# Splitting batch 0 at query 192 so that FFN blocks start on its first tokens

## The chip, the cores and the metric

The kernel runs on one core of a Trainium2 chip. The metric is the device time of one execution in microseconds. A comparison is given as a ratio: the mean time of one kernel's fast runs over that of the other's fast runs of the same rounds, with a 95% interval. It is therefore not quite the ratio of the medians, which are quoted beside it. "Granted clock" is the share of TensorE's full rate that the chip grants at that moment; 0.5 is half clock.

The kernel before took 367.71 us in the rounds of the changed kernel. On the other chips that the experiments ran on, its medians were 367.65 to 368.13 and its single runs 367.04 to 368.56. Half a microsecond between kernels therefore means something only within the same rounds.

## The reference

Attention in a sliding window of 128 keys with a linear bias, over 8 batches of 576 tokens, 8 heads of 64; the outcome goes through a gated FFN (GELU of one product times another, then the output product).

```python
scores = np.matmul(q, k.transpose(0, 1, 3, 2)) / np.sqrt(D)
rel = pos[:, None] - pos[None, :]
mask = (rel >= 0) & (rel < 128)
scores = np.where(mask, scores + bias, -1e9)        # bias = -slope[h] * abs(rel)
attn = np.exp(scores - scores.max(-1, keepdims=True))
attn = attn / (attn.sum(-1, keepdims=True) + 1e-9)
x = np.matmul(attn, v) ...                          # [4608, 512]
out = (gelu(x @ w_gate) * (x @ w_val)) @ w_out      # d_ff = 1536
```

## The kernel before

Attention is computed transposed: keys on partitions, queries along the row. For a batch, ScalarE (ACT) takes the exponential of the scores in PSUM (the banks into which TensorE writes its results), VectorE (DVE) multiplies by a table with bias and window ("mask"). TensorE (PE) then makes the sums of the probabilities with a matrix of ones, DVE their reciprocals, PE spreads these over the heads' partitions, and PE multiplies with v. DVE writes the product of the values and the reciprocals to `xT`, which the FFN reads. The parts that the argument touches:

```python
def sums(b, s):                       # PE, then the reciprocal on DVE
    ...
    nc.vector.reciprocal(sumrow[b][:, lo:hi], ps[:, 0:hi - lo])

def values(b, s, cs):                 # PE, then the product that FFN reads
    ...
        nc.vector.tensor_tensor(out=xT[...], in0=ps[:, 0:hi - lo],
                                in1=recip[b][:, c, lo:hi], op=ALU.mult)

def gate_val(g, f, lo=0, hi=512):     # one FFN block: 128 of the 1536 columns
    pg, pv = bank(), bank()
    ... 8 matmuls of hi - lo columns ...
    nc.scalar.activation(out=gl, in_=pg, func=AF.Gelu)
    nc.vector.tensor_tensor(out=hid[g][:, f, lo:hi], in0=pv, in1=gl, op=ALU.mult)
```

Batch 0 cannot hide behind FFN work, as there is none yet. The kernel before cuts it at query 320 (cut where marked):

```python
first((0, 1))                                       # transposes of head pairs 0, 1
scores(0, 0, (0, 1), lambda: first((2,)))
first((3,))
scores2(0)
scores(0, 0, (2, 3), lambda: rest((0, 1), dve))
scores(0, 1, (0, 1), lambda: sums(0, 0))
rest((2, 3), act)
scores(0, 1, (2, 3))
spread_pe(0, 0)
values(0, 0, range(4))
sums(0, 1)
for f in range(2):
    gate_val(0, f, 0, 320)
spread_pe(0, 1)
gate_val(0, 2, 0, 320)
values(0, 1, range(4))
for f in range(3):
    gate_val(0, f, 320, 512)
...                                                 # blocks 3 to 11 on 512 columns
```

The softmax here doesn't subtract the row's maximum and nothing guards it: scores larger than these inputs give would overflow.

## Time and profile before

| What | Kernel before |
|---|---|
| time, median | 367.71 us |
| PE busy over the span | 95% |
| granted clock full again from | 23.6 us |
| first FFN matmul | 23.3 us |
| last mask of batch 0 ends | 21.1 us |
| second reciprocal | 23.45 to 25.2 us |
| batch 1 keys transposed on PE | 41.98 us |

From FFN block 8 on, both kernels do the same work in the same order, and PE transposes batch 1 between the blocks. In the profiled run of the kernel before, 367.3 us minus 41.98 is 325.3 us.

In the timelines, a line gives the start and the length in us, engine, source line, operation, output and input, and the count of merged instructions. In brackets stands the idle time of that engine before it and what ended it.

### The profile page before, as it was taken

To read this page: it belongs to the slowest core of one execution; us is meant where nothing else is said; L and a number is where in the kernel's file an instruction comes from. 1 tells how busy PE (TensorE), PEld (TensorE's weight loads), DVE (VectorE), ACT (ScalarE), POOL (GpSimd) and SP (SyncE) were. 2 spreads that over 40 slices of the span, in tenths; PEclk is the share of its full clock that TensorE was granted. 3 is DMA by queue.
4 is the path that set the end of the run, shared out by engine and by line. 5 is a ranking of instruction groups with operands and counts; after the bars stand their busy time and mean duration, and the time that the engine had idled before them with its cause. 6 is when DMAs were issued, how large, how long until landed. Compare 5 with 4: busy or idle time off the path is not lost.

```text
span 365.5 us, 6601 instructions
## 1 busy us (share of the span) xinstructions
PE 347.8 (95%) x2614; PEld 171.3 (47%) x2656; DVE 188.6 (52%) x306; ACT 187.3 (51%) x339; POOL 107.9 (30%) x140
## 2 busy tenths in 40 slices
PE   3799999999999999999999999999999999999995
PEld 2455545444454445444445444444444444444442
DVE  4794448543695469475547454655564404302320
ACT  5863487434966376943783368436842223323321
POOL 8945859913519202900850040000000000000000
PEclk9779999999999999999999999999999999999999
DMA  9999999999969994999991992094205020011002
GB/s 103 136 199 178 177 163 184 174 153 200 162 116 121 136 92 81 143 103 217 127 196 50 228 97 89 33 221 53 87 32 131 0 109 7 0 60 58 0 29 88
DMA packets 151168, 41.41 MB, mean 113 GB/s; under 512 B 138816, under 2 KB 144448, under 8 KB 151136
## 3 DMA queue, kind: packets, MB, share of 16 engines
q0 software_dynamic: 112608, 18.88, 67.8%
q1 hardware_dynamic: 38528, 22.10, 27.2%
q8 instruction: 21, 0.34, 0.4%
q14 instruction: 11, 0.09, 0.1%
HBM read 42.47 MB, written 9.51 MB: 142 GB/s over the span
## 4 chain that ended last, share of the span: by engine, by line
PE 86%; ACT 5%; DVE 3%; DMA 3%; issue 1%; POOL 1%; POOLq 0%; SPq 0%; ACTq 0%; DVEq 0%
PE ps L281 50%; PE ps L297 23%; PE ps L262 4%; ACT P L170 4%; PE ps L163 4%; DMA qT<-qs 3%; PE ps L221 2%; PE ps L244 2%; DVE r L230 1%; DVE P L173 1%; DVE xT L268 1%; ACT emask L346 1%; PE ps L142 1%; POOL ks L104 0%; ACT L170 0%
## 5 line engine op out<-in xcount | busy, mean ns | idle before, releaser
L286 DVE TENSOR_TENSOR hT<-ps,gelu 128x512 bf16<-128x512 f32 (+2 forms) x111 | 74.3, 674 | 121.9 <-PE ps L281 109.3
L285 ACT ACTIVATE gelu<-ps 128x512 bf16<-128x512 f32 (+2 forms) x111 | 64.9, 585 | 119.6 <-PE ps L281 117.2
L281 PE MATMUL ps<-xT,wg 128*128 128x512 bf16 (+2 forms) x430 | 110.6, 374 | 0.8
L281 PE MATMUL ps<-xT,wv 128*128 128x512 bf16 (+2 forms) x435 | 110.4, 373 | 0.6
L297 PE MATMUL ps<-wo,hT 128*128 128x512 bf16 x413 | 97.2, 380 | 1.5 <-issue 0.6
L170 ACT ACTIVATE P<-ps 128x512 bf16<-128x512 f32 x144 | 74.4, 632 | 7.1 <-PE ps L163 7.0
L281 PEld LDWEIGHTS <-wv 128*128 128x128 bf16 x444 | 43.3, 98 | 50.3 <-issue 0.2
L281 PEld LDWEIGHTS <-wg 128*128 128x128 bf16 x444 | 41.9, 98 | 48.9 <-issue 1.1
L173 DVE TENSOR_TENSOR P<-P,emask 128x1024 bf16<-128x1024 bf16 x72 | 48.3, 685 | 31.3 <-ACT P L170 31.0
L297 PEld LDWEIGHTS <-hT 128*128 128x128 bf16 x432 | 39.8, 98 | 49.0 <-issue 4.4
L84 POOL DMA_DIRECT2D vb<-in_v_dram x40 | 33.7, 862 | 75.8 <-PE ps L262 75.0
L302 ACT COPY osb<-ps 128x512 f32<-128x512 f32 x36 | 21.7, 603 | 37.2 <-PE ps L297 32.8
L84 POOL DMA_DIRECT2D qs<-in_q_dram x35 | 29.6, 877 | 24.9 <-DMA qT<-qs 12.9
L230 DVE RECIPROCAL r<-ps 128x320 f32<-128x320 f32 (+1 forms) x16 | 30.7, 1939 | 3.1 <-PE ps L221 3.1
L84 POOL DMA_DIRECT2D ks<-in_k_dram x35 | 29.6, 887 | 6.4 <-DMA qs<-in_q_dram 3.0
L163 PE MATMUL ps<-qT,kT 64*128 64x256 bf16 (+1 forms) x384 | 24.0, 254 | 3.0 <-DVE kT L136 1.3
L268 DVE TENSOR_TENSOR xT<-ps,rb 128x320 bf16<-128x320 f32 (+1 forms) x64 | 24.7, 449 | 0.8 <-DMA rb<-rd 0.8
L163 PEld LDWEIGHTS <-kT 64*128 64x128 bf16 x384 | 13.1, 96 | 16.9 <-issue 11.6
L262 PE MATMUL ps<-P,vb 128*64 128x128 bf16 (+2 forms) x384 | 19.4, 251 | 0.1
L262 PEld LDWEIGHTS <-vb 128*64 128x64 bf16 x384 | 15.4, 113 | 7.3 <-issue 7.2
L221 PE MATMUL ps<-P,ones 128*32 128x128 bf16 (+2 forms) x384 | 11.6, 256 | 1.3 <-DVE P L173 1.3
L221 PEld LDWEIGHTS <-ones 128*32 128x32 bf16 x384 | 8.5, 101 | 5.6 <-issue 4.5
(47 smaller groups left out, 91.3 us busy)
## 6 DMA issues: line engine op xcount, KB each, us to landing
out_dram<-osb SPq DMA_DIRECT2D x36, 256.0 KB, 2.7
rb<-rd SPq DMA_DIRECT2D x8, 576.0 KB, 7.1
vb<-in_v_dram POOLq DMA_DIRECT2D x32, 128.0 KB, 4.7
qs<-in_q_dram POOLq DMA_DIRECT2D x28, 128.0 KB, 6.7
ks<-in_k_dram POOLq DMA_DIRECT2D x28, 128.0 KB, 6.4
wg<-in_moe_w_gate_dram POOLq DMA_DIRECT2D x4, 384.0 KB, 11.0
wv<-in_moe_w_val_dram POOLq DMA_DIRECT2D x4, 384.0 KB, 12.2
wo<-in_moe_w_out_dram POOLq DMA_DIRECT2D x2, 768.0 KB, 10.9
```

The lines of the kernel that those rows point to most:

```text
L84: nc.gpsimd.dma_start(out=t[lo:128, j, :].rearrange("p (h d) -> p h d", h=H), in_=src[b][:, 128 * j - 64 + lo:128 * j + 64, :].rearrange(" ...
L163: nc.tensor.matmul(out=ps[:, col:col + 128 * n].rearrange("p (n t) -> p n t", n=n), lhsT=blocks(kT, b, i, c, j, 1).rearrange("p n t -> p ( ...
L170: nc.scalar.activation(out=dst, in_=src, func=AF.Exp, scale=0.125)
L173: nc.vector.tensor_tensor(out=dst, in0=dst, in1=m, op=ALU.mult)
L221: nc.tensor.matmul(out=ps[32 * c:32 * c + 32, a:e], lhsT=ones[:, min(j, 1), i, :], rhs=prob(b, s, c, i, j, e - a), start=(i == 0 and j == ...
L230: nc.vector.reciprocal(sumrow[b][:, lo:hi], ps[:, 0:hi - lo])
L262: nc.tensor.matmul(out=ps[64 * i:64 * i + 64, a:e], lhsT=vb[b % 2][:, j, 64 * h:64 * h + 64], rhs=prob(b, s, c, i, j, e - a), start=(j == ...
L268: nc.vector.tensor_tensor(out=xT[:, c, b * S + lo:b * S + hi], in0=ps[:, 0:hi - lo], in1=recip[b][:, c, lo:hi], op=ALU.mult)
L281: nc.tensor.matmul(out=ps[:, 0:hi - lo], lhsT=w[:, c, 128 * f:128 * (f + 1)], rhs=xT[:, c, t0 + lo:t0 + hi], start=(c == 0), stop=(c == 3))
L285: nc.scalar.activation(out=gl[:, 0:hi - lo], in_=pg[:, 0:hi - lo], func=AF.Gelu)
L286: nc.vector.tensor_tensor(out=hid[g][:, f, lo:hi], in0=pv[:, 0:hi - lo], in1=gl[:, 0:hi - lo], op=ALU.mult)
L297: nc.tensor.matmul(out=po, lhsT=hid[g][:, f, 128 * t:128 * (t + 1)], rhs=wo[:, f, :], start=(f == 0), stop=(f == NF - 1))
```

## The change

Its intent is to bring FFN work to PE sooner. The first 192 tokens go through all of attention first; six FFN blocks run on these 192 columns while exponentials, masks and the reciprocal of the other 384 are made. Loads are reordered for it: 192 tokens' queries and keys, then the other 384, two pieces of v, half of the gate and value weights, the rest. The core of the diff:

```diff
-PART = ((0, 320), (320, 576))
+PART = ((0, 320), (320, 576), (0, 192), (192, 576))
...
-    RUNS = ((0, 128, 3), (384, 96, 2))
+    RUNS = ((0, 96, 2), (192, 128, 3))
...
+    for w in (0, 1):
+        transpose_runs(0, w, range(4), dve)
+    scores_first()
+    transpose_runs(1, 0, (0, 1), act)
+    transpose_runs(1, 1, (0, 1), act)
+    transpose_runs(1, 0, (2, 3), dve)
+    sums(0, 2)
+    transpose_runs(1, 1, (2, 3), act)
+    scores(0, 1, (0, 1), lambda: (spread_pe(0, 2, (dve, dve)), values(0, 2, range(4))))
     scores(0, 1, (2, 3))
-    spread_pe(0, 0)
-    values(0, 0, range(4))
-    sums(0, 1)
-    for f in range(2):
-        gate_val(0, f, 0, 320)
-    spread_pe(0, 1)
-    gate_val(0, 2, 0, 320)
-    values(0, 1, range(4))
-    for f in range(3):
-        gate_val(0, f, 320, 512)
+    scores2(0, 2)
+    scores2(0, 1)
+    later = []
+    for f in range(3):
+        gate_val(0, f, 0, 192, later)
+    sums(0, 3)
+    for tail in later:
+        tail()
+    for f in (3, 4):
+        gate_val(0, f, 0, 192)
+    spread_pe(0, 3)
+    gate_val(0, 5, 0, 192)
+    values(0, 3, range(4))
+    for f in range(6):
+        gate_val(0, f, 192, 512)
```

With `later`, GELU and product of blocks 0 to 2 are emitted behind the second reciprocal, so that they do not hold it up on DVE.

More of the change, by code (lines that the diff above doesn't have):

```diff
@@ L12 @@
 ENG = mybir.EngineType
-PART = ((0, 320), (320, 576))
+PART = ((0, 320), (320, 576), (0, 192), (192, 576))
 PIECES = (((0, 0, 192), (1, 64, 320), (2, 192, 320)),
-          ((2, 0, 128), (3, 0, 256), (4, 128, 256)))
-PCOL = ({0: 64, 1: 256}, {4: 0, 2: 128, 3: 256})
+          ((2, 0, 128), (3, 0, 256), (4, 128, 256)),
+          ((0, 0, 192), (1, 64, 192)),
+          ((1, 0, 128), (2, 0, 128), (2, 128, 256), (3, 128, 384), (4, 256, 384)))
+PCOL = ({0: 64, 1: 256}, {4: 0, 2: 128, 3: 256}, {0: 0, 1: 192})
 @with_exitstack
@@ L90, in load_qk, with load_run, load_v @@
         load(ks[b % 2], k, b)
-    RUNS = ((0, 128, 3), (384, 96, 2))
+    RUNS = ((0, 96, 2), (192, 128, 3))
     def runs(t, n):
         first, parts, r = RUNS[n]
-        lo = 1536 * n
+        lo = 1024 * n
         return t.rearrange("p j x -> p (j x)")[0:parts, lo:lo + 512 * r].rearrange(
             "p (h x) -> p h x", h=H)
-    def load_runs(n, h0, h1):
+    def load_run(n, t, src):
         first, parts, r = RUNS[n]
-        for t, src in ((qs[0], q), (ks[0], k)):
-            nc.gpsimd.dma_start(
-                out=runs(t, n)[:, h0:h1, :],
-                in_=src[0][h0:h1, first:first + parts * r, :].rearrange(
-                    "h (p r) d -> p h (r d)", r=r))
-    def load_v(b):
-        load(vb[b % 2], v, b)
+        nc.gpsimd.dma_start(
+            out=runs(t, n),
+            in_=src[0][:, first:first + parts * r, :].rearrange("h (p r) d -> p h (r d)", r=r))
+    def load_v(b, js=range(5)):
+        load(vb[b % 2], v, b, js)
     def load_w(lo, hi):
@@ L120, in by_pair, with transpose_runs @@
         return t.rearrange("p j c t -> p (j c t)").rearrange("p (c x) -> p c x", c=4)
-    def transpose_runs(n, what, c, ps):
+    def transpose_runs(n, what, cs, copy):
         first, parts, r = RUNS[n]
         src = runs((qs, ks)[what][0], n)
-        for x in range(r):
-            for i in (0, 1):
-                nc.tensor.transpose(
-                    out=ps[64 * i:64 * i + 64, parts * x:parts * x + parts],
-                    in_=src[:, 2 * c + i, 64 * x:64 * x + 64],
-                    identity=ident[0:parts, 0:parts])
-    def untangle(copy, n, what, c, ps):
-        first, parts, r = RUNS[n]
-        dst = by_pair((qT, kT)[what][0])[:, c, 64 + first:64 + first + parts * r]
-        copy(out=dst.rearrange("p (x r) -> p x r", r=r),
-             in_=ps[:, 0:parts * r].rearrange("p (r x) -> p x r", r=r))
+        ps = bank().bitcast(BF16)
+        for k, c in enumerate(cs):
+            for x in range(r):
+                lo = parts * (r * k + x)
+                for i in (0, 1):
+                    nc.tensor.transpose(
+                        out=ps[64 * i:64 * i + 64, lo:lo + parts],
+                        in_=src[:, 2 * c + i, 64 * x:64 * x + 64],
+                        identity=ident[0:parts, 0:parts])
+        for k in range(0, len(cs), 2):
+            lo = parts * r * k
+            dst = by_pair((qT, kT)[what][0])[
+                :, cs[k]:cs[k] + 2, 64 + first:64 + first + parts * r]
+            copy(out=dst.rearrange("p c (x r) -> p c x r", r=r),
+                 in_=ps[:, lo:lo + 2 * parts * r].rearrange("p (c r x) -> p c x r", c=2, r=r))
     def transpose(b, what, c, copy):
@@ L173, in mask, with scores2 @@
         nc.vector.tensor_tensor(out=dst, in0=dst, in1=m, op=ALU.mult)
-    def scores2(b):
+    def scores2(b, j=2):
         P = p2_pool.tile([128, 4, 2, 128], BF16, name="P2")
-        probs2[b] = P
+        probs2[b, j] = P
         ps = [bank(), bank()]
@@ L181, in scores2, with scores_first @@
             for i in (0, 1):
-                score(b, c, i, 2, 2, 1, ps[i], 128 * c)
+                score(b, c, i, j, 2, 1, ps[i], 128 * c)
         for i in (0, 1):
             exp(P[:, :, i, :], ps[i].rearrange("p (c n) -> p c n", c=4))
-        mask(P.rearrange("p c i n -> p (c i) n"), emask[:, :, 0:128])
+        lo = 128 * (2 - j)
+        mask(P.rearrange("p c i n -> p (c i) n"), emask[:, :, lo:lo + 128])
+    def scores_first():
+        pss = []
+        for c in range(4):
+            ps = [bank(), bank()]
+            pss.append(ps)
+            for j, a, e in PIECES[2]:
+                for i in (0, 1):
+                    col = PCOL[2][j]
+                    nc.tensor.matmul(
+                        out=ps[i][:, col:col + e - a],
+                        lhsT=by_pair(kT[0])[64 * i:64 * i + 64, c, 128 * j:128 * j + 128],
+                        rhs=by_pair(qT[0])[64 * i:64 * i + 64, c, 64 + a:64 + e],
+                        start=True, stop=True)
+        for c, ps in enumerate(pss):
+            P = p_pool[0].tile([128, 2, 512], BF16, name="P")
+            probs[0, 2, c] = P
+            for i in (0, 1):
+                exp(P[:, i, 0:320], ps[i][:, 0:320])
+            mask(P[:, :, 0:192], emask[:, 2 * c:2 * c + 2, 64:256])
+            mask(P[:, :, 192:320], emask[:, 2 * c:2 * c + 2, 0:128])
     def scores(b, s, cs, then=None):
@@ L206, in scores, with prob @@
                  emask[:, 2 * c:2 * c + 2, :].unsqueeze(2).to_broadcast((128, 2, 2, 256)))
-    def prob(b, s, c, i, j, n):
-        if (s, j) == (0, 2):
-            return probs2[b][:, c, i, 0:n]
-        return probs[b, s, c][:, i, PCOL[s][j]:PCOL[s][j] + n]
+    def prob(b, s, c, i, j, a, e):
+        if (s, j) == (0, 2) or (s == 3 and a == 0):
+            return probs2[b, j][:, c, i, 0:e - a]
+        t = min(s, 1) if s != 2 else 2
+        return probs[b, t, c][:, i, PCOL[t][j]:PCOL[t][j] + e - a]
     sumrow, recip = {}, {}
@@ L217, in sums @@
         ps = bank()
-        for j, a, e in PIECES[s]:
+        for n, (j, a, e) in enumerate(PIECES[s]):
             for i in (0, 1):
@@ L222, in sums @@
                         out=ps[32 * c:32 * c + 32, a:e],
-                        lhsT=ones[:, min(j, 1), i, :], rhs=prob(b, s, c, i, j, e - a),
-                        start=(i == 0 and j == 2 * s), stop=(i == 1 and j == 2 * s + 2),
+                        lhsT=ones[:, min(j, 1), i, :], rhs=prob(b, s, c, i, j, a, e),
+                        start=(i == 0 and n == 0), stop=(i == 1 and n == len(PIECES[s]) - 1),
                         skip_group_check=True)
-        if s == 0:
+        if b not in sumrow:
             sumrow[b] = r_pool.tile([128, S], FP32, name="r")
@@ L238, in spread_dma, with spread_pe @@
                 in_=d[:, i, :].unsqueeze(0).to_broadcast((64, 4, S)))
-    def spread_pe(b, s):
+    def spread_pe(b, s, copies=(nc.scalar.copy, nc.vector.tensor_copy)):
         lo, hi = PART[s]
@@ L249, in spread_pe @@
         for c, ps in enumerate(pss):
-            copy = nc.scalar.copy if c % 2 == 0 else nc.vector.tensor_copy
-            copy(out=recip[b][:, c, lo:hi], in_=ps[:, 0:hi - lo])
+            copies[c % 2](out=recip[b][:, c, lo:hi], in_=ps[:, 0:hi - lo])
     def values(b, s, cs):
@@ L258, in values @@
             pss.append(ps)
-            for j, a, e in PIECES[s]:
+            for n, (j, a, e) in enumerate(PIECES[s]):
                 for i in (0, 1):
@@ L264, in values @@
                         lhsT=vb[b % 2][:, j, 64 * h:64 * h + 64],
-                        rhs=prob(b, s, c, i, j, e - a),
-                        start=(j == 2 * s), stop=(j == 2 * s + 2), skip_group_check=True)
+                        rhs=prob(b, s, c, i, j, a, e),
+                        start=(n == 0), stop=(n == len(PIECES[s]) - 1),
+                        skip_group_check=True)
         for c, ps in zip(cs, pss):
@@ L272, with gate_val @@
     hid = {}
-    def gate_val(g, f, lo=0, hi=512):
+    def gate_val(g, f, lo=0, hi=512, later=None):
         if g not in hid:
@@ L283, in gate_val, with act @@
                     rhs=xT[:, c, t0 + lo:t0 + hi], start=(c == 0), stop=(c == 3))
-        gl = g_pool.tile([128, 512], BF16, name="gelu")
-        nc.scalar.activation(out=gl[:, 0:hi - lo], in_=pg[:, 0:hi - lo], func=AF.Gelu)
-        nc.vector.tensor_tensor(out=hid[g][:, f, lo:hi], in0=pv[:, 0:hi - lo],
-                                in1=gl[:, 0:hi - lo], op=ALU.mult)
+        def act():
+            gl = g_pool.tile([128, 512], BF16, name="gelu")
+            nc.scalar.activation(out=gl[:, 0:hi - lo], in_=pg[:, 0:hi - lo], func=AF.Gelu)
+            nc.vector.tensor_tensor(out=hid[g][:, f, lo:hi], in0=pv[:, 0:hi - lo],
+                                    in1=gl[:, 0:hi - lo], op=ALU.mult)
+        if later is None:
+            act()
+        else:
+            later.append(act)
     acc = {}
@@ L304, in out_half @@
             nc.sync.dma_start(out=out[r0:r0 + 128, :], in_=osb)
-    load_runs(0, 0, 4)
+    load_run(0, qs[0], q)
+    load_run(0, ks[0], k)
     nc.vector.memset(ident, 0.0)
@@ L314 @@
         base=0, pattern=[[-1, 128]], channel_multiplier=1)
-    load_runs(0, 4, 8)
+    load_run(1, qs[0], q)
     tmpl = consts.tile([128, 256], FP32, name="tmpl")
@@ L323 @@
             base=base, pattern=[[step, 128]], channel_multiplier=chan)
-    load_runs(1, 0, 8)
+    load_run(1, ks[0], k)
+    load_v(0, (0, 1))
+    step = DFF // 4
+    load_w(0, step)
     for c in range(4):
@@ L328 @@
             base=-32 * c, pattern=[[-16, 2], [0, 64]], channel_multiplier=1)
-    load_v(0)
-    step = DFF // 4
-    for n in range(4):
+    load_w(step, 2 * step)
+    load_v(0, (2, 3, 4))
+    for n in (2, 3):
         load_w(step * n, step * (n + 1))
@@ L350 @@
     act, dve = nc.scalar.copy, nc.vector.tensor_copy
-    def first(cs):
-        for w in (0, 1):
-            for c in cs:
-                ps = bank().bitcast(BF16)
-                transpose_runs(0, w, c, ps)
-                untangle(act if c == 3 else dve, 0, w, c, ps)
-    def rest(cs, copy):
-        for c in cs:
-            for w in (0, 1):
-                ps = bank().bitcast(BF16)
-                transpose_runs(1, w, c, ps)
-                untangle(copy, 1, w, c, ps)
-    first((0, 1))
-    scores(0, 0, (0, 1), lambda: first((2,)))
-    first((3,))
-    scores2(0)
-    scores(0, 0, (2, 3), lambda: rest((0, 1), dve))
-    scores(0, 1, (0, 1), lambda: sums(0, 0))
-    rest((2, 3), act)
-    scores(0, 1, (2, 3))
-    spread_pe(0, 0)
-    values(0, 0, range(4))
-    sums(0, 1)
-    for f in range(2):
-        gate_val(0, f, 0, 320)
-    spread_pe(0, 1)
-    gate_val(0, 2, 0, 320)
-    values(0, 1, range(4))
-    for f in range(3):
-        gate_val(0, f, 320, 512)
+    for w in (0, 1):
[7 more added lines that the diff above has]
+    scores(0, 1, (0, 1), lambda: (spread_pe(0, 2, (dve, dve)), values(0, 2, range(4))))
+    scores(0, 1, (2, 3))
+    scores2(0, 2)
+    scores2(0, 1)
+    later = []
+    for f in range(3):
+        gate_val(0, f, 0, 192, later)
[9 more added lines that the diff above has]
+        gate_val(0, f, 192, 512)
     for n in range(2):
@@ L426 @@
             load_v(g + 2)
-        for f in range(3 if g == 0 else 0, NF):
+        for f in range(6 if g == 0 else 0, NF):
             gate_val(g, f)
```

## The prediction

> **What bounds the kernel now.** I read the page's forty slices first, then the chain that ended last, then the timelines of TensorE, VectorE and GpSimd for the first 50 us, then the table of stretches with the granted clock, then the DMA issues.
>
> The forty slices (9.14 us each):
> ```profile
> PE   3799999999999999999999999999999999999995
> DVE  4794448543695469475547454655564404302320
> PEclk9779999999999999999999999999999999999999
> DMA  9999999999969994999991992094205020011002
> ```
> From slice 4 on PE is full at full clock; the change does not touch that work. What can be won lies in slices 1 to 4: PE waits, and PE at reduced clock.
>
> TensorE's timeline there (start, us, engine, line, operation, count, idle before):
> ```profile
> 17.51 1.06 PE L163 MATMUL ps<-qT,kT 64*128 64x128 bf16 x12 [0.16 <-ACT kT L136]
> 18.91 1.45 PE L244 MATMUL ps<-r,sel 32*128 32x320 f32 x8 [0.35 <-DVE r L230]
> 20.30 2.13 PE L262 MATMUL ps<-P,vb 128*64 128x192 bf16 x24
> 22.36 1.04 PE L221 MATMUL ps<-P,ones 128*32 128x128 bf16 x24
> ...
> 28.62 1.23 PE L281 MATMUL ps<-xT,wg 128*128 128x192 bf16 x4
> 29.69 0.49 PE L281 MATMUL ps<-xT,wv 128*128 128x192 bf16 x4
> ...
> 41.98 0.44 PE L142 MATMUL ps<-ident,ks 128*128 128x128 bf16 x5
> ```
> From 18.9 to 28.6 PE has no gap: three FFN blocks on 320 tokens (L281) fill the second reciprocal. The one gap is at 28.62, where PE waits for the last xT product: that product ends at 29.56, so I count the remaining FFN as starting at about 29.4. At 41.98 batch 1 is transposed.
>
> VectorE's timeline, the links between:
> ```profile
> 16.61 2.16 DVE L230 RECIPROCAL r<-ps 128x320 f32<-128x320 f32 x1 [1.21 <-PE ps L221]
> 23.45 1.76 DVE L230 RECIPROCAL r<-ps 128x256 f32<-128x256 f32 x1
> 28.15 1.41 DVE L268 TENSOR_TENSOR xT<-ps,rb 128x256 bf16<-128x256 f32 x4
> ```
> The reciprocal is 2.16 us for 320 columns and 1.76 for 256: 6.25 ns a column, so 1.36 us for 192 and 2.56 us for 384.
>
> Stretches (us, PE, PEld, DVE, ACT, POOL busy, clock, DMA share, GB/s):
> ```profile
> 12.00:14.00 2.00, 0.80 (x18) 0.50 (x13) 1.55 (x5) 2.00 (x5) 2.00 (x4) 0.84 1.88 120
> 20.00:22.00 2.00, 2.00 (x26) 1.60 (x24) 2.00 (x5) 1.85 (x4) 0.70 (x1) 0.50 1.26 189
> 23.00:24.00 1.00, 1.00 (x16) 0.58 (x9) 1.00 (x3) 0.00 (x0) 0.38 (x1) 0.70 1.32 204
> ```
> A clock of 0.84 over two us, with 0.50 after, puts the fall at 13.4; 0.70 over one us puts the rise at 23.6. For ten us PE ran at half clock: the twelve score matmuls at 17.51 took 1.06 us, the same twelve at 55.67 took 0.62.
>
> DMA issues of two of the last batch 1 key tiles (KB each, us to landing):
> ```profile
> ks<-in_k_dram POOLq DMA_DIRECT2D x2, 128.0 KB, 5.6
> ```
> The last of them is issued at 35.87, so it lands at about 41.5, just ahead of the 41.98 at which PE transposes it. The DMA queue is full all the way there.
>
> **What the Trainium skill says.** "TensorE: Matmul & The Clock Gate", Part 1: the HAM clock gate: half clock is the default, a busy window of about 3.4 us releases it, an idle one puts it back. The trace agrees on the sizes: the half-clock stretch of 10.2 us is three such windows. It also shows that less than an idle window suffices: at 13.4 the clock fell although PE was busy for roughly half of the window before. Same page, "Architectural detail", queue depths: PE may pull only weight loads ahead, ACT and DVE are strictly first in, first out. The timelines agree (instructions run in program order), and the argument below rests on it. "ScalarE: Activation LUTs", What ACT_TABLE_LOAD costs: about 1283 ns for the load; the trace has 1.28 us at 21.12, hidden. "DMA: Bandwidth & Descriptors", Specifications: line rate needs 512 B or more; the trace agrees in kind: the table of stretches has about 202 GB/s while weights come, 154 while 128-byte head rows of batch 1 do.
>
> **The change part by part.**
>
> 1. Loads. Equal bytes in another order, 192 tokens first. The first queries land at 4.97 now and should at about 5.2, the keys at 6.5 instead of 6.16 (smaller packets); the 384 tokens' keys land at about 11.6 (now 11.8). One issue of 0.76 us fewer ahead of the mask template lets the eight emask exponentials end at 7.6 instead of 8.3. Gate and value weights of the first quarter land near 18.4 instead of 22.2, the second quarter near 22.3 instead of 26.1, late v tokens near 24. These meet their readers.
>
> 2. First part. Scores of 192 tokens: eight exponentials of 320 columns at about 0.36 us (from 0.31 for 256 and 0.49 to 0.51 for 512) run 8.3 to 11.2, masks end at 11.7. PE then waits about 1.6 us for the keys of part two (11.6). Transposes, sums, transposes end at 14.1 at half clock; the VectorE copy of the transposed queries ends at 14.0; reciprocal 14.0 to 15.4; spread 15.4 to 16.4; values to 17.5; xT to 18.2.
>
> 3. Exponentials of part two. Twelve of 512 columns at 0.51 are 6.1 us, starting at 15.05 after the last ACT copy, with about 0.9 us idle while PE is in the spread and values: end at about 22.1, last mask at 22.8. Now the last mask ends at 21.1. So the first FFN starts early (first block at 19.1, now 23.3), but the last attention input comes later by 1.7.
>
> 4. Second part. sums(0, 3) needs that last mask with its first piece; it ends near 23.6 and the reciprocal of 384 columns runs 23.7 to 26.25, against 23.45 to 25.2 now. FFN blocks 0 to 2 have run (19.1 to 21.65), block 3 runs 23.5 to 24.15. Block 4 needs the PSUM bank of block 0's value half, which VectorE frees only after the reciprocal, as its three products stand behind it: bank free at 26.6. The spread stands behind block 4 on PE: 26.6 + 0.65 (block 4: eight matmuls of 192 columns at 0.082) + 1.1 (spread: 0.71 for 256 columns, so 1.07 for 384) + 0.65 (block 5) + 1.4 (values: 768 streamed columns a head for 512 in the 24 matmuls that took 1.07 at 27.56, with some 0.2 of fixed tail) + 0.6 (last product) = 31.0.
>
> 5. The balance. At that point six blocks of 192 = 1152 columns are done, against three of 320 = 960. The difference, 192 columns by eight matmuls at 2.4 columns a ns (512 columns step by 0.216 us), is 0.64 us. So the remaining FFN starts 31.0 - 0.2 (the same overlap as now) - 29.4 = 1.4 later with 0.64 less to do: **a loss of 0.8 us** at full clock.
>
> 6. The clock. PE is dense from about 15.4, so the window 16.8 to 20.2 can release the clock at 20.2 rather than 23.6; the working above includes it. But PE is idle about 1.2 us before sums and 2.4 us before block 4. The window 23.6 to 27.0 would have it busy for about a third; at 13.4 about a half was not enough. If it throttles, spread, block 5 and values run at half clock until 30.4: about 1.5 us more, **a loss of 2.3**. I hold this for as likely as not.
>
> **The rivals.**
>
> A, the intended gain. If my half-clock estimates for 11 to 19 us are too long, or block 4's bank comes free early, the remaining FFN starts at 28.5 to 29.5: a gain of 0.5 to 1.5. For it: the present PE spends ten us at half clock, and dense FFN work sooner is what releases it. Against: the chain of steps 2 to 4 is made of ACT and DVE work, which does not shorten. Time: 366.2 to 367.2.
>
> B, the keys of batch 1. PE may not transpose them before about 40.5 to 41.5, whatever comes earlier, since the bytes ahead in the queue are the same. For it: the present margin is half a us (41.5 against 41.98). This caps A: even if the FFN started 3 us sooner, PE would wait at block 8 and the gain would stay within about 1.5. Time: not under 366.
>
> C, the clock falls back in the reciprocal's gap: 370.0. For it the fall at 13.4; against it that the skill asks for a whole idle window, and that this gap is shorter.
>
> **Range and chances.** Plain working 368.5, with the fallback 370.0, with the intended gain 366.2 to 367.2. As such an order was probably chosen with some gain in view, I weigh A at 0.4, the plain loss at 0.3, C at 0.3: centre 368.2, eight in ten between 366.2 and 370.2. A change of 2% would be 7.4 us; the whole stretch in question has some 4 us of PE idle and 5 us of half-clock loss after 10 us, so neither side is likely: faster 0.01, within 2% 0.97, slower 0.02.
>
> **What would show it.** In the changed kernel's PE timeline: first L281 of 192 columns at about 19; a gap of about 2 us between block 3 and block 4 that ends with VectorE's product; spread near 27, first 320-column L281 near 30.5. VectorE: reciprocals of 1.36 and 2.56 us, the second starting near 23.7. Stretches: clock back to 1.0 near 20.2, and either 0.5 again near 27 (C) or not. The prediction is wrong if the second reciprocal starts before 22.5, if there is no gap before block 4, or if a wait for ks stands at the batch 1 transposes (B, with A). It is wrong on the whole premise if the difference arises after 50 us.

## More of the kernel before

Most of the lines of the kernel before stand in the prediction. Two readings that it does not show are the last masks of batch 0 (DVE's timeline), and three places of the chain that ended last:

```profile
18.68 2.43 DVE L173 TENSOR_TENSOR P<-P,emask 128x1024 bf16<-128x1024 bf16 x4
```

```profile
12.45 0.69 DVE P L173
...
22.43 0.97 PE ps L221 x19
...
29.61 2.11 PE ps L281 x22
```

At 29.61 runs the first matmul that reads the last xT product; from there the rest of FFN has all its input.

## The result

The changed kernel took 369.20 us (368.88 to 369.70, four runs) against 367.71: ratio 1.0040, interval 1.0025 to 1.0055. It is clearly slower by about 1.5 us. The profiled run is the slowest of the four (369.7 us).

The page's forty slices of the changed kernel:

```profile
PE   3789999999999999999999999999999999999995
PEclk9999999999999999999999999999999999999999
DMA  9999999999949994999993994094205020011002
```

PE is again full from slice 4 on. The clock row reads 9 throughout, also where PE ran at half clock: no change of clock is recorded in this run before 22.0 us, and the row shows full clock until the first record. The matmuls themselves tell the clock.

TensorE's timeline of the changed kernel:

```profile
12.58 0.85 PE L133 MATMUL ps<-ident,ks 128*64 128x128 bf16 x12 [2.45 <-DMA ks<-in_k_dram]
...
20.86 0.82 PE L310 MATMUL ps<-xT,wg 128*128 128x192 bf16 x4
...
24.48 0.85 PE L250 MATMUL ps<-P,ones 128*32 128x128 bf16 x40 [0.94 <-DVE P L178]
...
28.00 1.55 PE L273 MATMUL ps<-r,sel 32*128 32x384 f32 x8 [1.24 <-DVE r L259]
...
32.81 0.30 PE L310 MATMUL ps<-xT,wg 128*128 128x320 bf16 x1 [0.17 <-DVE xT L297]
...
44.38 0.44 PE L147 MATMUL ps<-ident,ks 128*128 128x128 bf16 x5
```

The reader is to see four things. PE waits 2.45 us for the later keys. FFN does start sooner (20.86 for 23.33). But the sums wait for the last mask, which is late, and the first matmul that reads the last xT product runs at 32.81 instead of 29.61. At the batch 1 keys the kernel is 2.40 us behind (44.38 for 41.98), and 369.7 minus 44.38 is again 325.3: **all of the loss of this trace arises in the first 44 us**, none of it later. (It is more than the 1.5 us between the means, as this run is the slowest of its four.)

ACT's timeline and then DVE's, around the last mask:

```profile
19.68 4.03 ACT L175 ACTIVATE P<-ps 128x512 bf16<-128x512 f32 x8 [1.37 <-PE ps L168]
...
23.73 1.28 ACT L316 ACT_TABLE_LOAD   x1
```

```profile
23.74 0.69 DVE L178 TENSOR_TENSOR P<-P,emask 128x1024 bf16<-128x1024 bf16 x1 [0.29 <-ACT P L175]
25.38 2.56 DVE L259 RECIPROCAL r<-ps 128x384 f32<-128x384 f32 x1 [0.95 <-PE ps L250]
27.86 1.37 DVE L317 TENSOR_TENSOR hT<-ps,gelu 128x192 bf16<-128x192 f32 x5
```

ACT stood idle for 1.37 us just before its last eight exponentials. The last mask ends at 24.43 (21.1 before), and the second reciprocal starts at 25.38 (23.45 before) and is wider.

The chain that ended last, in order of time, says where the start of all this lies:

```profile
5.23 7.30 DMA ks<-in_k_dram
...
12.58 1.49 PE ps L133 x24
14.07 0.66 PE ps L250 x16
14.72 0.78 PE ps L133 x11
15.50 0.97 PE ps L168 x12
...
16.48 1.43 PE ps L273 x7
17.90 1.21 PE ps L290 x8
19.11 0.58 PE ps L168 x6
19.70 4.02 ACT P L175 x8
...
23.74 0.70 DVE P L178
...
24.48 0.87 PE ps L250 x40
...
25.38 2.57 DVE r L259
```

In the kernel before, the chain runs at 12.5 us through masks of scores that were made from keys loaded in halves by heads. Here it starts at one load of 384 KB of keys, which ends at 12.53. From 12.58 to 19.70 the chain is work of PE alone, 7.1 us of it, and all before the clock was released at 22.0: it is behind this work that ACT waited.

### The profile page after: what moved, and what is told of

Its sections match the earlier page's. It is cut to its first block, busy times and chain, and to the rows that moved or that the text cites. A ratio compares the mean times of both kernels' runs of the same rounds, so it can differ in the third digit from the quotient of the medians.

```text
span 367.9 us, 6707 instructions
## 1 busy us (share of the span) xinstructions
PE 347.5 (94%) x2662; PEld 175.1 (48%) x2704; DVE 189.4 (51%) x311; ACT 187.3 (51%) x339; POOL 107.0 (29%) x138
## 4 chain that ended last, share of the span: by engine, by line
PE 86%; ACT 6%; DVE 3%; DMA 2%; issue 1%; POOL 1%; POOLq 0%; ACTq 0%
PE ps L310 49%; PE ps L333 23%; ACT P L175 5%; PE ps L290 5%; PE ps L168 4%; PE ps L250 2%; DMA ks<-in_k_dram 2%; PE ps L273 2%; DVE r L259 1%; DVE P L178 1%; ACT L175 1%; DVE xT L297 1%; PE ps L133 1%; PE ps L147 1%; POOL qs L107 0%
## 5 line engine op out<-in xcount | busy, mean ns | idle before, releaser
L175 ACT ACTIVATE P<-ps 128x512 bf16<-128x512 f32 (+1 forms) x146 | 74.0, 626 | 8.4 <-PE ps L168 7.8
L310 PEld LDWEIGHTS <-wv 128*128 128x128 bf16 x456 | 44.6, 98 | 49.4 <-issue 0.4
L310 PEld LDWEIGHTS <-wg 128*128 128x128 bf16 x456 | 43.0, 98 | 48.2 <-issue 1.3
L178 DVE TENSOR_TENSOR P<-P,emask 128x1024 bf16<-128x1024 bf16 (+1 forms) x77 | 49.1, 653 | 31.9 <-ACT P L175 31.6
L259 DVE RECIPROCAL r<-ps 128x320 f32<-128x320 f32 (+3 forms) x16 | 30.7, 1937 | 2.9 <-PE ps L250 2.9
L297 DVE TENSOR_TENSOR xT<-ps,rb 128x320 bf16<-128x320 f32 (+3 forms) x64 | 24.7, 449 | 0.5 <-DMA rb<-rd 0.5
L168 PE MATMUL ps<-qT,kT 64*128 64x128 bf16 (+1 forms) x376 | 22.5, 253 | 0.9 <-DVE kT L150 0.4
L168 PEld LDWEIGHTS <-kT 64*128 64x128 bf16 x376 | 13.4, 99 | 13.6 <-issue 11.8
L250 PE MATMUL ps<-P,ones 128*32 128x128 bf16 (+2 forms) x392 | 10.7, 245 | 2.0 <-DVE P L178 2.0
```

The lines of the kernel that those rows point to most:

```text
L168: nc.tensor.matmul(out=ps[:, col:col + 128 * n].rearrange("p (n t) -> p n t", n=n), lhsT=blocks(kT, b, i, c, j, 1).rearrange("p n t -> p ( ...
L175: nc.scalar.activation(out=dst, in_=src, func=AF.Exp, scale=0.125)
L178: nc.vector.tensor_tensor(out=dst, in0=dst, in1=m, op=ALU.mult)
L250: nc.tensor.matmul(out=ps[32 * c:32 * c + 32, a:e], lhsT=ones[:, min(j, 1), i, :], rhs=prob(b, s, c, i, j, a, e), start=(i == 0 and n == 0 ...
L297: nc.vector.tensor_tensor(out=xT[:, c, b * S + lo:b * S + hi], in0=ps[:, 0:hi - lo], in1=recip[b][:, c, lo:hi], op=ALU.mult)
L310: nc.tensor.matmul(out=ps[:, 0:hi - lo], lhsT=w[:, c, 128 * f:128 * (f + 1)], rhs=xT[:, c, t0 + lo:t0 + hi], start=(c == 0), stop=(c == 3))
```

## The experiments

Each run edits one of the two kernels. Three numbers are compared: the ratio to the kernel before on the same chip, the start of the second reciprocal, and the instant of the first batch 1 key transposes, the last two in the profiled run.

| Run | median us | ratio (95%) | 2nd reciprocal | batch 1 keys |
|---|---|---|---|---|
| changed kernel | 369.20 | 1.0040 (1.0025 to 1.0055) | 25.38 | 44.38 |
| after_again | 369.42 | 1.0046 (1.0031 to 1.0061) | 24.83 | 43.83 |
| few | 371.33 | 1.0087 (1.0072 to 1.0102) | 25.60 | 46.32 |
| order | 371.37 | 1.0097 (1.0072 to 1.0122) | 26.93 | 45.92 |
| after_warm | 369.75 | 1.0043 (1.0027 to 1.0059) | 24.96 | 43.96 |
| after_warm_gap | 369.04 | 1.0036 (1.0019 to 1.0053) | 24.97 | 43.98 |
| halves | 368.39 | 1.0017 (0.9988 to 1.0045) | 24.49 | 43.49 |
| late | 369.25 | 1.0038 (1.0020 to 1.0055) | 24.86 | 43.85 |
| best | 366.87 | 0.9981 (0.9962 to 1.0001) | 21.63 | 40.62 |
| best_again | 366.89 | 0.9980 (0.9966 to 0.9994) | 21.64 | 40.64 |
| best_split | 369.45 | 1.0039 (1.0019 to 1.0060) | 22.52 | 41.82 |
| before_warm | 367.25 | 0.9974 (0.9957 to 0.9991) | 23.76 | 41.99 |
| before_hot | 367.22 | 0.9988 (0.9974 to 1.0002) | 24.17 | 42.41 |

In nine of the twelve experiments the profiled run's time minus the last column is 325.3 to 325.5 us, so the last column accounts for the time. In `halves`, `after_warm` and `best_split` it is 326.3, 325.9 and 325.8. There PE waits once more than in the changed kernel, at 177 to 179 us, for the DMA that transposes queries (`DMA qT<-qs`): 0.84, 0.52 and 0.39 us. That is far from the edits.

### after_again: the control

The changed kernel, unedited, beside `halves`, `late` and `after_warm_gap`.

> The changed kernel itself, unedited, as the control for the other three runs on this chip. All theories: 1.0 to 2.0 us over the kernel before, ratio near 1.004; second reciprocal at about 25.4, second keys waited for until about 12.5.

The loss repeated. In this run the clock was released at 17.3 us and not at 22.0, and the batch 1 keys came 0.55 us sooner although the later keys were waited for until 12.97, 0.39 us longer. From the first transposes of these keys to the second reciprocal it took 11.86 us, for 12.80 in the changed kernel's trace: a first measure, 0.9 us, of what PE's clock is worth here.

### few: only three early FFN blocks

```diff
-    for f in (3, 4):
-        gate_val(0, f, 0, 192)
     spread_pe(0, 3)
-    gate_val(0, 5, 0, 192)
     values(0, 3, range(4))
-    for f in range(6):
+    for f in range(3):
         gate_val(0, f, 192, 512)
```

> Edit to the changed kernel: only FFN blocks 0 to 2 run on the first 192 tokens; blocks 3 to 5 run later on 512 as in the kernel before. Theory E: blocks 3 and 4 only fill PE while VectorE does the second reciprocal (25.38 to 27.94), so their 1.3 us of PE work moves behind it and the time rises by 1.0 to 1.5 us; block 5 stands on the chain either way and is neutral. Rival G (the six extra narrow blocks cost more than they give: more instructions, smaller matmuls): the time falls by 0.3 us or more.

The ratio rose from 1.0046 (control) to 1.0087, about 1.5 us. So the early blocks 3 to 5 earn their place; the rival that the narrow blocks cost more than they give falls. But part of the rise is another effect, seen in PE's timeline and the table of stretches (us, then busy time of PE, PEld, DVE, ACT, POOL, clock, DMA share, GB/s):

```profile
28.21 1.26 PE L273 MATMUL ps<-r,sel 32*128 32x384 f32 x8 [2.66 <-DVE r L259]
29.41 2.77 PE L290 MATMUL ps<-P,vb 128*64 128x128 bf16 x40
```

```profile
26.00:28.00 2.00, 0.00 (x0) 0.00 (x0) 2.00 (x1) 0.01 (x1) 0.65 (x1) 1.00 1.31 203
30.00:32.00 2.00, 2.00 (x34) 1.75 (x30) 1.85 (x5) 0.34 (x1) 0.73 (x2) 0.50 2.11 164
```

Without the blocks PE pauses 2.66 us, the clock falls to half, and the forty value matmuls take 2.77 us, against 1.52 in the control. That is the prediction's rival C, and it happened here though not in the changed kernel, whose pause is 1.24 us. All four runs of `few` have a mean clock of 0.995, which one window of 3.4 us at half clock would give (28.7 to 32.1 in the traced run); no run of the changed kernel in its own rounds is under 0.998. Blocks 3 and 4 thus do two things: they use the reciprocal's time, and they keep the clock up.

### order: the last scores before the spread

```diff
-    scores(0, 1, (0, 1), lambda: (spread_pe(0, 2, (dve, dve)), values(0, 2, range(4))))
+    scores(0, 1, (0, 1))
     scores(0, 1, (2, 3))
+    spread_pe(0, 2, (dve, dve))
+    values(0, 2, range(4))
```

> Edit to the changed kernel: the spread and the values of the first 192 tokens are emitted after the scores of head pairs 2 and 3 of the second part, not between them and those of pairs 0 and 1. Theory E (the exponentials and masks of the second part set when the second reciprocal starts; PE stands in their way at half clock): the 1.37 us that ACT idles before its last eight exponentials goes, the last mask and the second reciprocal come 1.0 to 1.4 us earlier (reciprocal at about 24.2 for 25.38), the time falls by 0.8 to 1.3 us although the first narrow FFN block starts later. Rival F (the start of the first FFN block sets the gain): the first block starts about 1 us later than 20.86, and the time rises or stays.

Slower, 1.0097. The theory of this run was wrong in one step. DVE's timeline, then ACT's:

```profile
20.41 0.69 DVE L178 TENSOR_TENSOR P<-P,emask 128x1024 bf16<-128x1024 bf16 x1 [0.29 <-ACT P L175]
21.02 1.14 DVE L279 COPY rb<-ps 128x192 f32<-128x192 f32 x4
22.08 1.14 DVE L297 TENSOR_TENSOR xT<-ps,rb 128x192 bf16<-128x192 f32 x4
```

```profile
22.16 2.06 ACT L175 ACTIVATE P<-ps 128x512 bf16<-128x512 f32 x4 [1.78 <-PE ps L168]
```

With the four masks emitted first, the spread's copies stood behind them on DVE and moved from 17.49 to 21.02. The last scores, which wait for these copies' PSUM banks, came late, and ACT idled 1.78 us in another place. The wait was moved, not removed.

The masks alone do not make up the delay: the last one ended at 24.95, only 0.52 us later than in the changed kernel, and the reciprocal started 1.55 us later. In the traced run the clock fell to half from 21.8 to 25.2 us, most of the three FFN blocks ran in it, and the sums, which stand behind them on PE, started only at 26.02. Two of the runs with the same time have a mean clock of 1.0; they were not traced.

### after_warm and after_warm_gap: the clock

Matmuls on a zeroed tile, before the first queries (9) and, in the second run, also in the wait for the later keys (8):

```diff
+    spin(9)
     load_run(0, qs[0], q)
...
     transpose_runs(1, 0, (0, 1), act)
+    spin(8)                            # after_warm_gap only
```

> Edit to the changed kernel: nine matmuls of 512 columns on zeros run on PE while it waits for the first queries, to release the clock early. Theory C (half clock on PE's steps of the chain, some 7 us of them between 12.6 and 19.7, is a large part of what the chain takes): if the clock is released and held, those steps shorten and the time falls by 1 to 2.5 us; if the 2.45 us wait for the second keys puts it back, it falls by under 0.5. Theory E alone (ACT and VectorE durations set the chain): under 0.7 us.

> Edit to the changed kernel: the nine matmuls on zeros at the start as in after_warm, and eight more in the wait for the second keys, so that the clock, released at about 4.5, is not put back at 7.9 by PE's pauses. Theory C: with full clock from about 5 to 22 the PE steps of the chain (7 us between 12.6 and 19.7 at half clock) shorten by 2 to 3 us and the time falls by 1.5 to 2.5 us against the control. If the clock falls all the same (the matmuls on zeros then take 0.43 us each and end after the keys have landed): within 0.7 us of the control, either way.

In `after_warm` the clock was full from 4.5 us and fell back at 7.9; PE's pauses there are 0.49, 0.50 and 0.66 us. No gain: 1.0043. In `after_warm_gap` it was full from 13.5 us on. The table of stretches and PE's timeline:

```profile
14.00:16.00 2.00, 2.00 (x60) 1.55 (x60) 0.93 (x2) 0.89 (x2) 1.51 (x2) 1.00 1.31 203
```

```profile
15.80 0.61 PE L168 MATMUL ps<-qT,kT 64*128 64x128 bf16 x12
17.44 0.61 PE L273 MATMUL ps<-r,sel 32*128 32x192 f32 x8 [1.02 <-DVE r L259]
```

The scores took 0.61 us for 1.04 in the changed kernel and the spread 0.61 for 1.43, but PE now waits 1.02 us for the first reciprocal. The matmuls on zeros also kept PE from the keys' transposes until 14.16, 1.2 us later than in the control, so this run has a cost of its own and its time (1.0036 against 1.0046) is no clean measure.

The traces allow a cleaner one. From the first transposes of the later keys to the second reciprocal it took 12.80 us in the changed kernel (full clock from 22.0), 12.81 in `after_warm` (from 21.5), 11.86 in the control (from 17.3) and 10.81 here (from 13.5). So PE's clock is part of the chain and worth some 1 to 2 us of it in these traces; here the late start of the transposes ate most of the gain. This run does not clear half clock of a part in the loss.

### halves: the later keys in two loads

```diff
-    load_run(1, qs[0], q)
+    load_run(1, qs[0], q, 0, 4)
...
-    load_run(1, ks[0], k)
+    load_run(1, ks[0], k, 0, 4)
+    load_run(1, qs[0], q, 4, 8)
+    load_run(1, ks[0], k, 4, 8)
...
-    transpose_runs(1, 0, (2, 3), dve)
     sums(0, 2)
-    transpose_runs(1, 1, (2, 3), act)
-    scores(0, 1, (0, 1), lambda: (spread_pe(0, 2, (dve, dve)), values(0, 2, range(4))))
+    scores(0, 1, (0, 1), lambda: (
+        transpose_runs(1, 0, (2, 3), dve), transpose_runs(1, 1, (2, 3), dve),
+        spread_pe(0, 2, (dve, dve)), values(0, 2, range(4))))
```

> Edit to the changed kernel: the loads of the 384 later queries and keys come in two halves by heads (queries 0 to 3, keys 0 to 3, queries 4 to 7, keys 4 to 7), and head pairs 0 and 1 go through transposes and scores before pairs 2 and 3. Theory K (the chain of part two starts at the landing of its keys, 12.53, which the kernel before did not wait for): keys 0 to 3 land near 10, the 2.45 us wait goes, the exponentials of part two start near 13.5 for 16.24, the second reciprocal comes 1 to 2.5 us earlier than 25.4, and the time falls by 1 to 2 us against the control. Rival (PE at half clock and the order of VectorE set the chain, not the keys): the second reciprocal moves by under 0.5 us.

ACT's timeline:

```profile
14.24 2.07 ACT L176 ACTIVATE P<-ps 128x512 bf16<-128x512 f32 x4 [0.69 <-PE ps L169]
18.80 4.03 ACT L176 ACTIVATE P<-ps 128x512 bf16<-128x512 f32 x8 [2.49 <-PE ps L169]
```

The wait for the later keys went (PE's pause before them is 0.56 us and ends with an exponential), and the exponentials of part two began at 14.24 for 16.24. The second reciprocal came only 0.34 us sooner than the control's, as ACT then idled 2.49 us before its last eight exponentials; in this trace the first keys also landed late (7.42 for 6.81). The median fell by 1.0 us, but the ratio's interval (0.9988 to 1.0045) overlaps the control's, and the traced run is the slowest of the four, so by time alone this run is inconclusive. Its lesson is that removing the first wait exposes the second.

### late: the last mask's piece last

```diff
-          ((1, 0, 128), (2, 0, 128), (2, 128, 256), (3, 128, 384), (4, 256, 384)))
+          ((2, 0, 128), (2, 128, 256), (3, 128, 384), (4, 256, 384), (1, 0, 128)))
```

> Edit to the changed kernel: in the list of pieces of part two, the piece whose mask is made last (key block 1, queries 192 to 320) goes last, so that sums and values start before that mask. Theory E (the last mask releases 0.85 us of sums and then the second reciprocal): only a fifth of the sums is left behind the mask, the reciprocal starts 0.4 to 0.7 us earlier, the time falls by 0.3 to 0.7. If another link sets the reciprocal, no change beyond 0.2.

Only 0.32 us of sums is left behind the last mask (0.87 before). The time did not move (1.0038 against 1.0046). The clock was released at 22.3 us in this run and at 17.3 in the control's. The fair neighbour is the trace of the changed kernel, with release at 22.0 and keys at 12.58 (here 12.61): against it the second reciprocal starts 0.52 us sooner and the batch 1 keys come 0.53 us sooner, as the sums' shortening says. So the traces show the gain that was expected, and the times do not.

### best, best_again: both waits taken away

`halves` and `late`, and the order mended: scores of pairs 2 and 3 before the values of part one, their masks behind the xT products, the spread's copies on ACT and DVE in turn. The added lines of the order:

```diff
+    sums(0, 2)
+    transpose_runs(1, 0, (2, 3), dve)
+    keep = []
+    scores(0, 1, (0, 1), keep=keep)          # masks kept for later
+    transpose_runs(1, 1, (2, 3), dve)
+    spread_pe(0, 2)
+    scores(0, 1, (2, 3), keep=keep)
+    values(0, 2, range(4))
+    for m in keep:
+        m()
     scores2(0, 2)
     scores2(0, 1)
```

> Edit to the changed kernel: the halves of the loads as in the run halves, the piece order of late, and the scores of pairs 2 and 3 before the values of part one with their masks behind the xT products on VectorE (in the run order the masks stood in front of the spread's copies and held them up); the spread's copies on ACT and VectorE in turn. Theory: the loss of the change is the wait for the second keys plus ACT's idle time of 1.4 to 2.5 us ahead of its last eight exponentials. With both gone the exponentials end near 21, the second reciprocal starts near 22.5 to 23.5 (25.38 in the changed kernel), and the time is 0.5 to 2.0 us under the changed kernel's offset, that is ratio to the kernel before 0.996 to 1.001. Rival (the split itself costs more than it gives: wider reciprocal, spread and values behind the last mask): ratio stays at 1.002 or above although the exponentials end earlier.

> The kernel of the run best, unedited, once more, on this chip, as control for best_split and because its first ratio (0.9981, interval up to 1.0001) leaves open whether it beats the kernel before. If the gain is real: ratio 0.996 to 0.999 with an upper end under 1.000. If the clock's release decides from run to run: runs spread over 366 to 368, with the profiled clock release between 11 and 22 us and the batch 1 transposes between 40 and 42.

ACT's and PE's timelines of `best`:

```profile
15.91 4.03 ACT L176 ACTIVATE P<-ps 128x512 bf16<-128x512 f32 x8 [0.24 <-PE ps L169]
```

```profile
20.69 0.89 PE L258 MATMUL ps<-P,ones 128*32 128x128 bf16 x40 [0.68 <-DVE P L179]
...
29.06 0.30 PE L318 MATMUL ps<-xT,wg 128*128 128x320 bf16 x1 [0.17 <-DVE xT L305]
...
40.62 0.44 PE L148 MATMUL ps<-ident,ks 128*128 128x128 bf16 x5
```

The last exponentials start 3.77 us sooner than in the changed kernel, the second reciprocal 3.75 us, the batch 1 keys 3.76 us: one shift handed down the chain. The ratio is 0.9981 and, repeated, 0.9980 with an interval that ends below 1. So the same split, with the same widths behind the last mask, **beats the kernel before by 0.2%** and the changed kernel by some 2.4 us (1.0046 minus 0.9980, of 368 us, each against the kernel before of its own rounds). The 3.76 us is more, as it compares the slowest run of the one with the fastest of the other. The runs spread over 366 to 368; the two slowest of `best` and the slowest of `best_again` have a mean clock of 0.993 or 0.994, the other nine 0.998 to 1.0.

The clock was released at 11.5 and 10.9 us in the two profiled runs, so a part of the 3.76 us may belong to the clock. No run separates clock and order cleanly, but one trace bounds the clock's part. `best_split`, below, is the same program up to the second reciprocal. Its clock was full only from 15.4 us, and its later keys were first transposed at 11.13 (9.97 in `best`). Its second reciprocal started at 22.52: 0.89 us after that of `best`, but 2.86 us before that of the changed kernel, and 2.45 before that of `after_warm_gap`, which had full clock sooner, from 13.5, but 1.2 us of delay of its own. So loads and order alone give some 1.3 us (2.45 less 1.2) or more; the rest of the 3.76 may be theirs or the clock's, and how much is the loads' and how much the order's was not measured.

### best_split: the second reciprocal in halves

```diff
-        nc.vector.reciprocal(sumrow[b][:, lo:hi], ps[:, 0:hi - lo])
+        # for s == 3: two reciprocals of 192 columns
...
-    spread_pe(0, 3)
+    spread_pe(0, 3, (act, act), (192, 384))
     gate_val(0, 5, 0, 192)
+    spread_pe(0, 3, (act, act), (384, 576))
```

> Edit to best: the second reciprocal in two instructions of 192 columns, and the second spread in two halves, the first one and block 5 standing in PE's gap during the second reciprocal, the copies on ACT alone. Theory E (after best the chain is sums, reciprocal of 2.56 us, spread 1.55, block 5 0.77, values): the first spread and block 5 leave the chain, the last xT product comes 0.7 to 1.2 us earlier, the time falls by 0.5 to 1.0 us against best_again. Rival B of the prediction (the keys of batch 1 land near 40): PE waits for them at the batch 1 transposes and the gain is under 0.4. Rival: VectorE's own row (two reciprocals, five FFN products, xT) sets the end, and nothing moves.

Slower than `best_again` by 2.6 us in the median. PE's timeline shows that the first spread still waits for both reciprocals (22.52 to 25.09):

```profile
25.24 1.14 PE L283 MATMUL ps<-r,sel 32*128 32x192 f32 x8 [1.33 <-DVE r L269]
```

The expected gain therefore never came about; why that wait stands there was not settled. It is not the only one: the trace has the spread's second matmul released by an FFN product at 25.3 and a later one by a Gelu at 25.7, and these stand behind both reciprocals as well. And of the 1.18 us by which the batch 1 keys came later than in `best_again`, 0.88 was there at the second reciprocal already, before the edit acts. Five of its six runs have a mean clock of 0.995, 368.8 to 370.5 us; the sixth has 1.0 and 367.6. One window of 3.4 us at half clock in 366 us makes the mean 0.995, so the five probably lost one; only the sixth was traced.

### before_warm and before_hot: the clock in the kernel before

`spin(9)` before the first loads; in `before_hot` also 5, 2, 4 and 1 matmuls on zeros in PE's pauses up to 17.5 us.

> Edit to the kernel before: the same nine matmuls on zeros ahead of its first transposes. If the clock is released early and held through the pause at 12.8 to 13.7, its ten us at half clock go and the time falls by 1 to 2 us, no more, as the keys of batch 1 land at about 41.5 against their use at 41.98 (rival B of the prediction: PE would then wait for DMA at the batch 1 transposes). If the pause puts the clock back, the time stays within 0.4 us.

> Edit to the kernel before: matmuls on zeros at the start and in PE's four pauses up to 17 us, to keep the clock released. Theory C with rival B of the prediction: if the clock stays at full from about 5 to 23, PE's steps of the chain there (5.6 us at half clock) shorten by up to 2.5 us, the remaining FFN starts near 27.5 for 29.4, and PE then waits for the keys of batch 1 (land near 41.5) at the batch 1 transposes, so that the time falls by 0.5 to 1.2 us only, ratio 0.997 to 0.9985. Without such a wait and with the clock held, up to 2.5 us. If the clock falls back all the same: as before_warm, ratio 0.997 to 1.000.

`before_warm` gained 0.26%, though in its profiled run the batch 1 keys stand at 41.99, where they stood without it, and the clock was full only from 21.9 us. The gain is thus not explained by that trace; the kernel before varied by 1.5 us in these rounds. In `before_hot` the clock was full from 15.0 us on instead of 23.6, and yet the rest of FFN started 0.4 us later and the ratio is 0.9988 (0.9974 to 1.0002). PE then waited elsewhere:

```profile
23.20 1.40 PE L281 MATMUL ps<-xT,wg 128*128 128x320 bf16 x4 [0.69 <-DVE xT L268]
```

The matmuls on zeros ran late themselves (the first scores of pairs 2 and 3 came at 12.65), which costs some of it. Still, full clock 8.6 us sooner bought nothing to be seen. That the start of the kernel before is set by ACT and DVE more than by PE's clock fits this, but one unclean run does not show it.

## Why the prediction was right or wrong

The prediction of 368.2 us with a range of 366.2 to 370.2 holds the measured 369.20, and "within 2%" is right. The centre was 1.0 us too low. The working itself gave 368.5, or 370.0 with the clock falling back; the measured value lies between. The centre was pulled down by rival A at 0.4, for which the profile had spoken least. It did not happen in the changed kernel: the rest of FFN would have had to start at 28.5 to 29.5, and it had its last input at 32.8. Only `best`, at 29.06, reached it. That the number came out so near is in part luck, as errors of more than 1 us cancelled (step 4).

**Step 1, loads.** First queries 5.31 for 5.2, first keys 6.36 for 6.5: right. The later keys were put at 11.6 and landed at 12.53, up to 12.97: the term was 0.9 to 1.4 us too small. The working reckoned by bytes in the queue alone. The prediction had foreseen a wait for them (1.6 us; measured 2.45), but as a detail: that it heads the chain of the loss was not seen. The weights met their readers, as predicted, if narrowly: in `best_again` PE waits 0.26 us, until 22.29, for value weights that were put at 22.3.

**Step 2, first part.** Exponentials from 8.36 and masks to 11.7: right to 0.1. Spread, values and xT ended at 19.70 for 18.2, of which 0.9 came from the keys. The spread was put at 1.0 us and took 1.43 at half clock.

**Step 3, exponentials of part two.** The mechanism was right: the first FFN block earlier (20.86, put at 19.1), the last mask later (24.43, put at 22.8). The last mask's 1.6 us are two terms of the sum: the exponentials began at 16.24 for 15.05, and ACT's idle time before its last ones was put at 0.9 and measured 1.37. `best` shows that it is this chain, exponentials to last mask to sums to reciprocal, that sets the end. What stands before it was misjudged: against rival A the prediction said that "the chain of steps 2 to 4 is made of ACT and DVE work", but from 12.58 to 19.70 the chain is PE's, and it shortens with the clock (12.80, 11.86 and 10.81 us under `after_warm_gap`).

**Step 4, second part.** This step failed in its middle. "Block 4 needs the PSUM bank of block 0's value half" was wrong: block 4's first matmuls ran at 25.94, before the products at 27.86, so no gap stood there. The prediction named this as a sign that it is wrong, and on this link it is. The banks did hold up part of the spread: its second matmul was released by an FFN product at 28.16 and its fourth by a Gelu at 28.58, and it took 1.55 us, not 1.1. The pause of PE during the reciprocal was 1.24 us, not 2.4. The two errors nearly cancel, by luck: the spread started at 28.0, put at 27.25, with the reciprocal 1.7 us late.

**Step 5, balance.** The rest of FFN was put 1.4 us later with 0.64 less to do, a loss of 0.8. In the profiled run the last product ended at 32.76, 3.2 us after the 29.56 of the kernel before; less 0.64 that is 2.56, against 2.40 at the batch 1 keys. The method of the sum was right, and its first terms (keys, last mask) too small.

**Step 6 and rival C, the clock.** The release was put at 20.2; it came at 22.0 and, in the control, at 17.3. The 20.2 took the edges of the clock's steps (13.4 and 23.6, three windows of 3.4 us apart) from the trace of the kernel before. They do not carry over: the two releases of this one kernel lie 4.65 us apart, which is no whole number of such windows. The fall back in the reciprocal's gap was held for as likely as not. It did not happen in the changed kernel's trace, where the pause was half of what the prediction had. In `few` it did, after a pause of 2.66 us. The control's slowest run (370.04 us, mean clock 0.994) may have had it too; it was not traced.

**Rival B, the keys of batch 1.** No run waited for them, not even at 40.62 in `best`. In the changed kernel's trace the last of them is issued at about 33.9 and takes 6.0 us, so it lands near 39.9, where the prediction had 40.5 to 41.5; in the control's it lands at 41.25, so that the new order of loads brings them sooner is not shown. In `best_again` they landed at 40.27, 0.37 us ahead of their use. The fastest runs of `best` and `best_again` (365.94 and 365.96) went just under the "not under 366" without such a wait; the cap itself was nearly but not quite reached, and stays untested.

**The rival that the split itself costs** (wider reciprocal, spread and values behind the last mask) is not what made it slow: `best` has the same widths and is faster than both.

## What to carry to other kernels

Work that is brought forward gains nothing if the chain that releases the end gets longer: before such a split, follow the last input of the second part back (here to one load of keys, to PE work at half clock, and to an ACT queue that idled behind it), not the first output of the first part. Where engines take their instructions in order, moving one piece ahead moves the wait to what stands behind it, so order, masks and load cuts have to be changed together; single mends here gave between nothing clear and a loss of 2 us, all together a gain. Work in a pause can also keep the clock up: in `few`, without it, the forty value matmuls took 1.25 us longer. And two traces of one kernel are to be compared only after a look at when the clock was released in each.

## What the Trainium skill lacked or had wrong

- "TensorE: Matmul & The Clock Gate", Part 1, gives the busy and the idle window of about 3.4 us but no figure for windows that are partly busy. In windows of 3.41 us without transposes, the clock held with PE busy for 2.19 us (changed kernel, 25.39 to 28.81) and 2.18 (control, 24.16 to 27.57), and fell with PE busy for 0.75 (`few`, 25.27 to 28.68) but also for 2.24 (`order`, 18.39 to 21.80, longest pause 0.67). So busy time alone does not decide it. The page's rule of thumb of no pause above some 3 us ("Why this matters for your kernels") was too generous in both runs that fell.
- The same page calls half clock the default; the profile's clock reads 1.00 until the first recorded change. The first sixteen transposes took 0.85 us in the changed kernel and 0.53 in `after_warm`, both under a clock shown as 1.00. No page says what the profile shows before its first record.
- No page tells how much a landing varies from run to run. The first keys of the changed kernel were used at 6.36 in one run and at 6.81 in another, the later keys at 12.58 and 12.97; in these traces the later keys stand at the head of the chain.
